# The first product of a channel MLP by one level of Strassen's algorithm, on chunks of 768 tokens

## The chip, the cores and the metric

The kernel runs on one core of a Trainium2 chip. A core has a matrix engine (TensorE, PE in the profile, with its weight loads as PEld), a vector engine (VectorE, DVE), a scalar engine (ScalarE, ACT), GpSimd (POOL) and a queue that issues transfers (SyncE, SP). Matmuls write to PSUM, which has eight banks of 512 floats per partition; everything else works in SBUF; DMA moves data between SBUF and HBM. The metric is the time of one execution on the device in microseconds (us), the median of several.

## The reference

The kernel computes attention, a gated mixer and a channel MLP for 4 batches of 576 tokens with 512 channels. The change concerns the MLP, which comes last (x is the output of the mixer):

```
mu = np.mean(x, axis=-1, keepdims=True)
var = np.mean((x - mu) ** 2, axis=-1, keepdims=True)
xn = (x - mu) / np.sqrt(var + 1e-06) * g_ln
ch = np.maximum(xn @ w_ch1, 0.0) @ w_ch2
return (x + ch).astype(np.float32)
```

w_ch1 is 512 x 2048 and w_ch2 2048 x 512. The weights arrive as 64-bit floats.

## The kernel before

Batches go through four segments each: "v" (5 steps), "u", "g" and "y" (8 steps each), in the order of `order` (L833). In g the gating product ps_g is multiplied with u (L569) and split (L570, L571); in y the output product ps_y gets its residual (L588) and goes to `y_scratch` in HBM (L590). A table of hooks places other work in front of a step: `hook(b, seg, i, fn)`. In the last batch these are weight pieces for the MLP (WA_AT, WC_AT) and the statistics of its first chunk (NORM0_AT). A hook gives a place in the written order, not a time: the framework's scheduler follows that order as a priority and may put a ready instruction of a later step before one that waits. On the chip each engine then keeps the order that it was given.

Every large product is made from float32r parts. `split` (L175) writes a high part on ACT and the rest on DVE, and `mm3` (L202) issues three matmuls for each 128 x 128 weight block: low by high, high by low, high by high. A weight load belongs to each matmul.

Weights are converted from 64 bits by `from_f64` (L184): ACT takes the scaled absolute value of the high word, DVE shifts it, puts the sign in (L194) and ORs the low word's bits (L196). Nine of the 32 pieces (PRE) are converted in an earlier batch and kept in `w_scratch`; `load_w` (L624) fetches or converts a piece and splits it into w1 or w2 tiles, which stay in SBUF for all chunks. g_ln is multiplied into w1 there.

The MLP has its tokens in five chunks (CUTS): two of 384, three of 512. `norm` (L658) has four steps for a chunk: load and sum over channels (step 0), subtract the mean and split into xn (1), the variance (2) and its inverse root, which is kept in rb (2 or 3). `ch1` (L736) makes one block of 128 features (4 blocks of channels by 3 matmuls, then Relu on ACT, L748, and the rest on DVE, L749), `ch2_mm` (L752) adds it to four accumulators, and `ch2_out` (L760) multiplies by rb, adds the residual and stores. The second product runs two blocks behind the first (LAG). For the first two chunks the features go in two halves, so that the later weights can be prepared meanwhile:

```
    todo = [(c, f, r, r + hh - 1) for r in (0, hh) for c in (0, 1) for f in range(r, r + hh)]
    todo += [(c, f, 0, NF - 1) for c in range(2, NCHUNK) for f in range(NF)]
```

PSUM: two banks hold ps_h, two the statistics, four the accumulators.

Of the kernel before, what the change touches and what calls it, by code (L numbers as in the profile page):

```python
# [24 lines left out]
P = 128  # L25
# [15 lines left out]
CUTS = (0, 384, 768, 1280, 1792, 2304)  # L41
CM = 512
NT = B * S
WP = 512
# [3 lines left out]
LAG = 2  # L48
# [10 lines left out]
WA_AT = (("u", 2), ("u", 2), ("u", 6), ("g", 2), ("g", 4), ("g", 5))  # L59
NORM0_AT = (("g", 0), ("g", 5), ("y", 5), ("y", 7))  # L60
WC_AT = (2, 5, 6, 6)
NORM1_AT = (1, 2, 6, 7)
NORM2_AT = (10, 11, 14, 15)
NORMC_AT = (5, 6, 9, 11)
# [3 lines left out]
PRE = (7, 8, 18, 21, 22, 24, 25, 28, 30)  # L68
# [12 lines left out]
NCHUNK = len(CUTS) - 1  # L81
TPC = CUTS[1] // P
# [65 lines left out]
def mixer_kernel(ctx: ExitStack, tc: tile.TileContext, io, out):  # L148
    nc = tc.nc
    y_d = nc.dram_tensor("y_scratch", (KD, P, NT), F32, kind="Internal").ap()  # L150
    w_d = nc.dram_tensor("w_scratch", (len(PRE), P, WP), F32, kind="Internal").ap()
    pools = {}
# [31 lines left out]
    def from_f64(raw, w, src, k, queue=nc.sync, after=None):  # L184
# [409 lines left out]
    wstage = []  # L594
# [25 lines left out]
    def from_pre(w, n):  # L620
        nc.sync.dma_start(out=w.bitcast(F32), in_=w_d[n])
        return w.bitcast(F32)

    def load_w(pl, i, j):  # L624
        k = wseq.index((i, j))
        w = wstage[0].tile([P, WP], U32, tag="w", name="w")
        if k in PRE:
            f = from_pre(w, PRE.index(k))
        else:
            raw = wstage[0].tile([P, 2 * WP], U32, tag="raw", name="raw")  # L630
            f = from_f64(raw, w, w_src(i, j), 2).rearrange("p k f -> p (k f)")
        if j < 2:
            if j == 0:
                w1[i] = pl.tile([P, 2, KD, 256], F32R, name=f"w1_{i}")
            kk = 2 * j
            f = f.rearrange("p (k f) -> p k f", k=2)
            for n in range(2):
                split(w1[i][:, 0, kk + n, :], w1[i][:, 1, kk + n, :], f[:, n, :],
                      scale=g_2[:, kk + n:kk + n + 1])
        else:  # L640
            if j == 2:
                w2[i] = pl.tile([P, 2, 2, DM], F32R, name=f"w2_{i}")
            j -= 2
            split(w2[i][:, 0, j, :], w2[i][:, 1, j, :], f)

    ys, xns, rbs, hs, accs = {}, {}, {}, {}, {}

    nst = {}

# [238 lines left out]
```

## Time and profile before

| | |
|---|---|
| median of 3 runs | 703.49 us (702.27 to 705.4) |
| the profiled execution, first to last instruction | 706.4 us |
| PE busy in it | 686.8 us, 97% |
| DVE, ACT busy | 59%, 40% |
| bytes moved by DMA | 61.25 MB |
| first matmul of the MLP | 300.66 us |

The profile is of one execution, which lies 0.4% above the median of the runs shown. Times in its rows count from the first instruction. Matmuls overlap: the distance between their starts tells what one costs, their listed duration includes the time that results take to come out. PE at 97% says that PE hardly waits, not that its matmuls could not be fewer.

### The profile page before, as it was taken

Reading aid. Unit: us, or ns where it says so; the run is one execution under the profiler, and the core shown is the slowest. Engines: PE = TensorE matmul, PEld = TensorE weight load, DVE = VectorE, ACT = ScalarE, POOL = GpSimd, SP = SyncE. Lnnn points to the kernel's source line nnn. Section 1 sums busy time; section 2 is a strip of 40 time slices with the busy share of each in tenths; the row PEclk is TensorE's granted clock in tenths of the full one; section 3 lists DMA queues with packets and bytes.
Section 4 is the critical chain, followed back from the end, with each engine's and each line's share of the span. In section 5 each row is a group of like instructions: output and inputs, shape, how many; then the busy total and the mean of one; then the engine's idle time right before and its main releaser. Section 6 shows DMA issues by size and latency. Waiting matters only on the chain.

```text
span 706.4 us, 11932 instructions
## 1 busy us (share of the span) xinstructions
PE 686.8 (97%) x4818; PEld 613.9 (87%) x4818; DVE 414.9 (59%) x866; ACT 280.9 (40%) x723; POOL 25.5 (4%) x26
## 2 busy tenths in 40 slices
PE   5999999999999999999999999999999999999997
PEld 4779979989998999999999999888888888888885
DVE  4889797696877894898963145656115461141113
ACT  3878966392578453465531114132111321111110
POOL 0012011000200020000000000000000000000000
PEclk9999999999999999999999999999999999999999
DMA  8764233457343524154420030300003000010001
GB/s 266 246 191 143 82 94 112 154 159 226 112 131 105 146 82 156 59 154 153 150 90 1 0 105 1 104 1 1 0 1 119 1 1 0 1 61 0 1 0 60
DMA packets 29240, 61.25 MB, mean 87 GB/s; under 512 B 3009, under 2 KB 10177, under 8 KB 29185
## 3 DMA queue, kind: packets, MB, share of 16 engines
q1 hardware_dynamic: 29184, 60.49, 27.2%
q8 instruction: 38, 0.62, 0.4%
q14 instruction: 18, 0.14, 0.1%
HBM read 48.68 MB, written 11.80 MB: 86 GB/s over the span
## 4 chain that ended last, share of the span: by engine, by line
PE 72%; DVE 10%; ACT 8%; DMA 6%; issue 1%; POOL 1%; SPq 1%; ACTq 0%; POOLq 0%; DVEq 0%
PE ps_h L205 9%; PE ps_h L203 9%; PE ps_h L204 9%; PE ps_o L203 8%; PE ps_o L204 8%; PE ps_o L205 8%; DMA w_scratch<-w_p 3%; ACT pt L400 2%; PE ps_y L203 2%; DMA yT<-y_scratch 2%; PE ps_y L204 2%; PE ps_y L205 2%; PE ps_t L439 1%; PE ps_v L203 1%; PE ps_pv L458 1%
## 5 line engine op out<-in xcount | busy, mean ns | idle before, releaser
L749 DVE SCALAR_TENSOR_TENSOR h<-ps_h,h 128x512 fp32r<-128x512 f32 (+1 forms) x80 | 50.6, 632 | 181.3 <-ACT h L748 181.2
L748 ACT ACTIVATE h<-ps_h 128x512 fp32r<-128x512 f32 (+1 forms) x80 | 44.3, 553 | 235.4 <-PE ps_h L205 230.0
L203 PE MATMUL ps_o<-h,w 128*128 128x512 f32 (+1 forms) x320 | 117.5, 368 | 0.3 <-DVE o L763 0.3
L203 PE MATMUL ps_h<-xn,w 128*128 128x512 f32 (+1 forms) x320 | 117.6, 367 | 0.0
L204 PE MATMUL ps_h<-xn,w 128*128 128x512 f32 (+1 forms) x320 | 117.5, 367 | 0.0
L205 PE MATMUL ps_h<-xn,w 128*128 128x512 f32 (+1 forms) x320 | 117.5, 367 | 0.0
L205 PE MATMUL ps_o<-h,w 128*128 128x512 f32 (+1 forms) x320 | 117.5, 367 | 0.0
L204 PE MATMUL ps_o<-h,w 128*128 128x512 f32 (+1 forms) x320 | 117.5, 367 | 0.0
L203 PEld LDWEIGHTS ps_o<-h,w 128*128 128x128 f32 x320 | 60.1, 188 | 8.6 <-DVE o L763 1.0
L204 PEld LDWEIGHTS ps_o<-h,w 128*128 128x128 f32 x320 | 60.0, 188 | 7.6
L205 PEld LDWEIGHTS ps_h<-xn,w 128*128 128x128 f32 x320 | 60.1, 188 | 7.5
L205 PEld LDWEIGHTS ps_o<-h,w 128*128 128x128 f32 x320 | 60.1, 188 | 7.5
L204 PEld LDWEIGHTS ps_h<-xn,w 128*128 128x128 f32 x320 | 60.1, 188 | 7.4
L203 PEld LDWEIGHTS ps_h<-xn,w 128*128 128x128 f32 x320 | 60.1, 188 | 7.4
L203 PE MATMUL ps_g<-wsg,vn 128*128 128x288 f32 x128 | 39.2, 307 | 0.3 <-ACT wsg L177 0.3
L203 PE MATMUL ps_y<-gt,wout 128*128 128x288 f32 x128 | 38.0, 298 | 1.1 <-ACT gt L570 1.1
L205 PE MATMUL ps_g<-wsg,vn 128*128 128x288 f32 x128 | 38.3, 300 | 0.0
L203 PE MATMUL ps_u<-xhl,winl 128*128 128x288 f32 x128 | 38.1, 297 | 0.0
L204 PE MATMUL ps_g<-wsg,vn 128*128 128x288 f32 x128 | 37.8, 296 | 0.0
L204 PE MATMUL ps_y<-gt,wout 128*128 128x288 f32 x128 | 37.7, 295 | 0.0
L205 PE MATMUL ps_u<-xhl,winh 128*128 128x288 f32 x128 | 37.7, 295 | 0.0
L205 PE MATMUL ps_y<-gt,wout 128*128 128x288 f32 x128 | 37.7, 295 | 0.0
(171 smaller groups left out, 1277.2 us busy)
## 6 DMA issues: line engine op xcount, KB each, us to landing
raw<-in_w_ch SPq DMA_DIRECT2D x23, 512.0 KB, 3.9
qk<-in_qk_s SPq DMA_DIRECT2D x8, 601.0 KB, 4.8
raw_p<-in_w_ch SPq DMA_DIRECT2D x18, 256.0 KB, 3.1
y_scratch<-y SPq DMA_DIRECT2D x16, 288.0 KB, 3.4
qk<-in_qk_l SPq DMA_DIRECT2D x7, 592.0 KB, 4.9
st<-in_w_in SPq DMA_DIRECT2D x8, 512.0 KB, 6.0
vt<-in_v_l SPq DMA_DIRECT2D x8, 432.0 KB, 5.4
vt<-in_v_s SPq DMA_DIRECT2D x8, 384.0 KB, 3.2
```

The lines of the kernel that those rows point to most:

```text
L203: nc.tensor.matmul(ps, lhsT=ll, rhs=rh, start=first, stop=False)
L204: nc.tensor.matmul(ps, lhsT=lh, rhs=rl, start=False, stop=False)
L205: last_mm[0] = nc.tensor.matmul(ps, lhsT=lh, rhs=rh, start=False, stop=last)
L400: exps.append(nc.scalar.activation(p3[:, i, :], src, AF.Exp, scale=SCALE, bias=mx[:, i:i + 1], accum_out=sm[:, i:i + 1]))
L439: nc.tensor.transpose(ps[:rows, (t - t0) * c:(t - t0 + 1) * c], src, ident)
L458: nc.tensor.matmul(ps[64 * h:64 * h + 64, (i - b0) * QB:(i - b0 + 1) * QB], lhsT=vt[:LW, (i * 2 + h) * D:(i * 2 + h + 1) * D], rhs=pT[:LW, ...
L748: nc.scalar.activation(h[:, 0, :], o, AF.Relu)
L749: nc.vector.scalar_tensor_tensor(out=h[:, 1, :], in0=o, scalar=0.0, in1=h[:, 0, :], op0=ALU.max, op1=ALU.subtract)
```

## The change

The tokens come in three chunks of 768 (TC), each in two halves of 384 (TH); a pair of feature blocks (256 columns of w_ch1) is the unit of the first product. The 512 channels are two halves as well, so that one pair is a 2 x 2 by 2 x 2 block product, and Strassen's algorithm (in Winograd's form) makes it from seven products of half the contraction instead of eight. WX names which of seven weight operands and which of seven token operands each product takes. `combine` makes the weight operands of a pair with four additions and three splits, `expand` the token operands with four subtractions and seven splits. `pair` issues the products in the order 1, 6, 2, 7, 4, 5, 3, adds them up on DVE, and gives the two blocks of the first half at once (h1, h2) and the two of the second half as sums kept in SBUF (`late`), whose Relu and second product come in a loop after the eight pairs. The second product of the first half stands between the products of the next pair.

w1 operands are 3.5 blocks of 512 columns in two parts, 1792 KB a pair, and only two pairs fit: each pair is written to `w1_scratch` once (`keep`) and read again for the second and third chunk (`fetch`). g_ln is now multiplied into the tokens (norm step 5). The inverse root is worked out with one reciprocal and a Newton step (`rsqrt`). The sign of the 64-bit weights comes from Prelu's slope, which saves one DVE operation in every conversion. Other pieces are converted early (PRE), and the hooks of the last batch change (PREP_AT, NORM0_AT). Banks: the pairs' products use one set of four banks, the accumulators of the first half the other, and the sets change places from chunk to chunk (role).

```diff
-CUTS = (0, 384, 768, 1280, 1792, 2304)
-CM = 512
+TC, TH = 768, 384
...
+WX = {1: (0, 0), 2: (1, 1), 7: (2, 5), 4: (3, 2), 5: (4, 3), 6: (5, 4), 3: (6, 6)}
...
-WA_AT = (("u", 2), ("u", 2), ("u", 6), ("g", 2), ("g", 4), ("g", 5))
-NORM0_AT = (("g", 0), ("g", 5), ("y", 5), ("y", 7))
...
+PREP_AT = (("u", 2, 2), ("u", 6, 1), ("g", 2, 2), ("g", 4, 1), ("g", 5, 2), ("y", 2, 1), ("y", 4, 2), ("y", 6, 1))
+NORM0_AT = (("g", 0, "n", 0), ("g", 3, "n", 1), ("g", 4, "n", 2), ("g", 6, "n", 3), ("g", 7, "n", 4), ("y", 1, "n", 5),
+            ("y", 2, "e", 0), ("y", 2, "e", 1), ("y", 3, "e", 2), ("y", 4, "e", 3), ("y", 5, "e", 4), ("y", 6, "e", 5),
+            ("y", 7, "e", 6))
+NORM_AT = ({6: (0, 1), 7: (2, 3, 4, 5)}, {2: (0,), 3: (1,), 4: (2,), 5: (3,), 6: (4,), 7: (5,)})
+EXPAND_AT = (0, 1, 3, 5, 6, 8, 10)
...
-PRE = (7, 8, 18, 21, 22, 24, 25, 28, 30)
+PRE = (8, 9, 12, 13, 16, 17, 20, 21, 24)
...
+    w1_d = nc.dram_tensor("w1_scratch", (NW, P, 14 * 2 * P), F32, kind="Internal").ap()
...
-        first = nc.scalar.activation(wf, high.bitcast(F32), AF.Abs, scale=F64_SCALE)
+        first = nc.scalar.activation(wf, high.bitcast(F32), AF.Prelu, scale=F64_SCALE, alpha=F64_SIGN)
...
         nc.vector.tensor_scalar(out=w, in0=w, scalar1=3, scalar2=None, op0=ALU.logical_shift_left)
-        nc.vector.scalar_tensor_tensor(out=w, in0=high, scalar=0x80000000, in1=w,
-                                       op0=ALU.bitwise_and, op1=ALU.bitwise_or)
         nc.vector.scalar_tensor_tensor(out=w, in0=low, scalar=29, in1=w,
                                        op0=ALU.logical_shift_right, op1=ALU.bitwise_or)
...
+    def piece(i, j):
...
         if k in PRE:
-            f = from_pre(w, PRE.index(k))
+            nc.sync.dma_start(out=w.bitcast(F32), in_=w_d[PRE.index(k)])
...
+            r0 = 1024 * (piece_turn[0] % 2)
+            piece_turn[0] += 1
+            from_f64(stg[:, r0:r0 + 1024], w, w_src(i, j), 2)
...
+    def combine(i):
...
+        tt(out=s[:, 0], in0=a21, in1=a22, op=ALU.add)
+        tt(out=s[:, 1], in0=s[:, 0], in1=a11, op=ALU.subtract)
+        tt(out=a21, in0=a11, in1=a21, op=ALU.subtract)
+        tt(out=s[:, 2], in0=a12, in1=s[:, 1], op=ALU.subtract)
+        w = w1[i] = big["w1", i % 2].tile([P, 2, 7, 2, P], F32R, tag="w1", name=f"w1_{i % 2}")
+        for src, j, m in ((wf[:, :, 0:P], 0, 2), (wf[:, :, P:2 * P], 2, 2), (s.rearrange("p s k f -> p (s k) f"), 4, 3)):
+            split(w[:, 0, j:j + m].rearrange("p s k f -> p (s k) f"), w[:, 1, j:j + m].rearrange("p s k f -> p (s k) f"),
+                  src)
...
+    def keep(i):
+        nc.sync.dma_start(out=w1_d[i], in_=w1[i].rearrange("p a s k f -> p (a s k f)").bitcast(F32))
+    def fetch(i):
+        w = w1[i] = big["w1", i % 2].tile([P, 2, 7, 2, P], F32R, tag="w1", name=f"w1_{i % 2}")
+        nc.sync.dma_start(out=w.rearrange("p a s k f -> p (a s k f)").bitcast(F32), in_=w1_d[i])
...
+    def second(i):
...
+        w = w2[i] = big["w2", i].tile([P, 2, 2, DM], F32R, name=f"w2_{i}")
+        split(w[:, 0].rearrange("p k f -> p (k f)"), w[:, 1].rearrange("p k f -> p (k f)"), f)
...
+    units = [(fn, a) for i in range(NW) for fn, a in (
+        (piece, (i, 0)), (piece, (i, 1)), (combine, (i,)), (piece, (i, 2)), (piece, (i, 3)), (second, (i,)))]
+    done = [0]
+    def prepare(n):
+        for fn, a in units[done[0]:done[0] + n]:
+            fn(*a)
+        done[0] += n
...
+    def bank(role, name):
+        if role:
+            return ps_d.tile([P, 512], F32, tag="d", name=name)
+        turns[0] += 1
+        if turns[0] % 2:
+            return ps_s.tile([P, 512], F32, tag="s", name=name)
+        return ps_a.tile([P, 512], F32, tag="a", name=name)
...
+    def norm(sc, step, role):
...
+            n = big["norm", 0] if sc == 0 else big["yc"].tile([P, KD * TC], F32, tag="yc", name="yc")
+            yc = ys[sc] = n[:, :KD * TC].rearrange("p (k t) -> p k t", k=KD)
+            nc.sync.dma_start(out=yc, in_=y_d[:, :, sc * TC:(sc + 1) * TC].rearrange("k p t -> p k t"))
...
+        if step in (1, 2):
+            half = step - 1
...
+            sr = col_sum(sc, half, False)
+            mean = bank(role, "ps_m")[:, :TH]
...
+                out=yc[:, :, cs], in0=mean.unsqueeze(1).to_broadcast([P, KD, TH]), scalar=-1.0 / DM,
+                in1=yc[:, :, cs], op0=ALU.mult, op1=ALU.add)
+        elif step in (3, 4):
+            half = step - 3
+            sr = col_sum(sc, half, True)
+            o = bank(role, "ps_v2")[:, :TH]
...
+            nc.scalar.activation(rbs[sc][:, half, :], o, AF.Identity, scale=1.0 / DM, bias=eps)
...
+            for k in range(KD):
+                nc.scalar.activation(yc[:, k, :], yc[:, k, :], AF.Copy, scale=g_2[:, k:k + 1])
...
+    def rsqrt(sc, half):
...
+        nc.scalar.activation(t, ve, AF.Sqrt)
+        nc.vector.reciprocal(r, t)
+        nc.scalar.activation(t, r, AF.Square)
+        nc.vector.tensor_tensor(out=t, in0=t, in1=ve, op=ALU.mult)
+        nc.vector.tensor_scalar(out=t, in0=t, scalar1=-0.5, scalar2=1.5, op0=ALU.mult, op1=ALU.add)
+        nc.vector.tensor_tensor(out=ve, in0=r, in1=t, op=ALU.mult)
...
+    def expand(sc, step):
+        yc = ys[sc]
+        b11, b12, b21, b22 = yc[:, 0:2, :TH], yc[:, 0:2, TH:], yc[:, 2:4, :TH], yc[:, 2:4, TH:]
...
+        def put(j, src):
+            x = xns[sc, j] = big["x"].tile([P, 2, 2, TH], F32R, tag=f"x{j}", name=f"x{j}")
+            split(x[:, 0], x[:, 1], src)
+        if step == 0:
+            put(0, b11)
+            tt(out=b11, in0=b12, in1=b11, op=ALU.subtract)
+        elif step == 1:
+            put(6, b22)
+            tt(out=b12, in0=b22, in1=b12, op=ALU.subtract)
         elif step == 2:
...
+            tt(out=b22, in0=b22, in1=b11, op=ALU.subtract)
+            put(4, b22)
+        elif step == 3:
+            put(1, b21)
+            tt(out=b21, in0=b22, in1=b21, op=ALU.subtract)
+        elif step == 4:
+            put(5, b12)
+        elif step == 5:
+            put(2, b21)
+        else:
+            put(3, b11)
+    def product(sc, i, o, m, first):
+        wj, xj = WX[m]
+        w, x = w1[i], xns[sc, xj]
+        for k in range(2):
+            for n, (a, c) in enumerate(((1, 0), (0, 1), (0, 0))):
+                nc.tensor.matmul(o, lhsT=w[:, a, wj, k, :], rhs=x[:, c, k, :], start=first and k == 0 and n == 0,
+                                 stop=k == 1 and n == 2, skip_group_check=True)
...
+    def to_h(src):
...
+    def ch2(sc, half, f, role, f0=0, f1=NF - 1, ds=range(KD)):
...
+    def leave(sc, half, d):
...
+        r = big["tmp"].tile([P, TH], F32, tag="o", name="o", bufs=2)
+        nc.vector.tensor_tensor(out=r, in0=accs[half, d][:, :TH], in1=rbs[sc][:, half, :], op=ALU.mult)
+        y = ys.pop((sc, half, d))
         nc.vector.tensor_tensor(out=y, in0=r, in1=y, op=ALU.add)
...
+        nc.sync.dma_start(out=out[d, :, cs], in_=y)
...
+    def pair(sc, i, role):
+        tt = nc.vector.tensor_tensor
+        f1, f2 = 2 * i, 2 * i + 1
+        a = bank(role, "ps_p1")[:, :TH]
+        product(sc, i, a, 1, True)
+        s1 = tmp("s1")
+        nc.scalar.activation(s1, a, AF.Copy)
+        b = bank(role, "ps_p6")[:, :TH]
+        product(sc, i, b, 6, True)
+        u2 = tmp("u2")
+        tt(out=u2, in0=b, in1=s1, op=ALU.add)
+        product(sc, i, a, 2, False)
+        h1 = to_h(a)
+        d = bank(role, "ps_p7")[:, :TH]
+        product(sc, i, d, 7, True)
+        u3 = tmp("u3")
+        tt(out=u3, in0=d, in1=u2, op=ALU.add)
+        if i:
+            ch2(sc, 0, f1 - 2, 1 - role)
+        e = bank(role, "ps_p4")[:, :TH]
+        product(sc, i, e, 4, True)
+        c21 = tmp("c21")
+        tt(out=c21, in0=u3, in1=e, op=ALU.subtract)
+        h2 = to_h(c21)
+        c = bank(role, "ps_p5")[:, :TH]
+        product(sc, i, c, 5, True)
+        tt(out=late(f2), in0=c, in1=u3, op=ALU.add)
+        if i:
+            ch2(sc, 0, f2 - 2, 1 - role)
+        product(sc, i, c, 3, False)
+        tt(out=late(f1), in0=c, in1=u2, op=ALU.add)
+        hs[f1], hs[f2] = h1, h2
+    def last_stage():
+        for sc in range(NSC):
+            role = sc % 2
+            for i in range(NW):
+                pair(sc, i, role)
+                if sc == 0:
+                    if i + 2 < NW:
+                        prepare(len(units[done[0]:]) if i + 3 == NW else 6)
+                        if i < NW - 2:
+                            keep(i + 2)
+                elif i + 2 < NW:
+                    fetch(i + 2)
+                if sc + 1 < NSC:
+                    for step in NORM_AT[sc > 0].get(i, ()):
+                        norm(sc + 1, step, role)
+                if i == NW - 3:
+                    residual(sc, 0)
+                if i >= NW - 2:
+                    rsqrt(sc, i + 2 - NW)
+            for f in (NF - 2, NF - 1):
+                ch2(sc, 0, f, 1 - role)
+            for d in range(KD):
+                leave(sc, 0, d)
+            if sc + 1 < NSC:
+                fetch(0)
+                fetch(1)
+            for f in range(NF):
+                hs[f] = to_h(late(f))
+                if sc + 1 < NSC and f in EXPAND_AT:
+                    expand(sc + 1, EXPAND_AT.index(f))
+                if f == 4:
+                    residual(sc, 1)
+                if f < NF - 2 or sc + 1 < NSC:
+                    ch2(sc, 1, f, role)
+            for d in range(KD):
+                if sc + 1 == NSC:
+                    for f in (NF - 2, NF - 1):
+                        ch2(sc, 1, f, role, ds=(d,))
+                leave(sc, 1, d)
...
     def open_c():
         close("mid")
...
+        right("x")
...
+    for seg, i, n in PREP_AT:
+        hook(last, seg, i, prepare, n)
+    for seg, i, what, step in NORM0_AT:
+        if what == "n":
+            hook(last, seg, i, norm, 0, step, 0)
+        else:
+            hook(last, seg, i, expand, 0, step)
+    hook(last, "y", 7, keep, 0)
...
+    open_d()
+    prepare(max(0, 12 - done[0]))
+    keep(1)
+    last_stage()
...
```

## Rows read from the trace of the kernel before

**Rows 1.** The page: the head and part 1, busy us, share and instructions.

```profile
span 706.4 us, 11932 instructions
PE 686.8 (97%) x4818; PEld 613.9 (87%) x4818; DVE 414.9 (59%) x866; ACT 280.9 (40%) x723; POOL 25.5 (4%) x26
```

**Rows 2.** Busy time by stretch: PE, PEld, DVE, ACT, POOL, PE clock, DMA share, GB/s.

```profile
269.00:278.00 9.00, 9.00 (x71) 9.00 (x70) 3.05 (x7) 1.30 (x3) 0.00 (x0) 1.00 0.61 206
...
285.50:300.66 15.16, 14.09 (x106) 13.85 (x105) 13.88 (x34) 7.27 (x13) 1.05 (x1) 1.00 0.23 79
300.66:360.00 59.34, 59.00 (x342) 58.36 (x341) 54.83 (x108) 33.29 (x62) 1.29 (x1) 1.00 0.49 156
360.00:700.00 340.00, 338.94 (x1597) 293.12 (x1597) 121.02 (x159) 61.38 (x92) 0.00 (x0) 1.00 0.06 22
```

**Rows 3.** Timeline of PE, first and last of three runs: start, duration, instruction.

```profile
292.07 0.29 PE L203 MATMUL ps_y<-gt,wout 128*128 128x288 f32 x1
...
294.05 0.30 PE L203 MATMUL ps_y<-gt,wout 128*128 128x288 f32 x1
...
307.28 0.33 PE L203 MATMUL ps_o<-h,w 128*128 128x384 f32 x1
...
311.44 0.33 PE L203 MATMUL ps_o<-h,w 128*128 128x384 f32 x1
...
690.10 0.39 PE L203 MATMUL ps_o<-h,w 128*128 128x512 f32 x1
...
695.54 0.39 PE L203 MATMUL ps_o<-h,w 128*128 128x512 f32 x1
```

**Rows 4.** Groups by line and shape, weight loads: count, busy us, mean ns, idle.

```profile
L203 PEld LDWEIGHTS ps_h<-xn,w 128*128 128x128 f32 x320 | 60.1, 188 | 7.4
```

**Rows 5.** Waits of PE: us in total, times, longest.

```profile
PE ps_m L673 <- DVE sr L178: 2.0, 2, 1.1
...
PE ps_y L203 <- ACT gt L570: 1.1, 1, 1.1
```

**Rows 6.** Timeline of DVE as the first chunk's tokens arrive.

```profile
276.33 0.56 DVE L653 TENSOR_TENSOR s<-yT 128x384 f32<-128x384 f32 x1 [2.84 <-DMA yT<-y_scratch]
276.80 0.55 DVE L654 TENSOR_TENSOR s<-yT 128x384 f32<-128x384 f32 x1
277.27 0.45 DVE L571 TENSOR_TENSOR gt<-z,gt 128x288 fp32r<-128x288 f32 x1
277.64 0.55 DVE L655 TENSOR_TENSOR s<-s,s 128x384 f32<-128x384 f32 x1
...
281.33 1.75 DVE L676 SCALAR_TENSOR_TENSOR xc<-ps_m,yT 128x1536 f32<-128x1536 f32 x1
283.00 0.45 DVE L571 TENSOR_TENSOR gt<-z,gt 128x288 fp32r<-128x288 f32 x1
```

**Rows 7.** Groups by line and shape: sign operation, reciprocal, table loads.

```profile
L194 DVE SCALAR_TENSOR_TENSOR w<-raw,w 128x512 uint32<-128x512 uint32 x23 | 15.8, 686 | 0.2
...
L699 DVE RECIPROCAL rb<-sd 128x512 f32<-128x512 f32 x3 | 10.1, 3353 | 10.0 <-ACT sd L696 10.0
...
L288 ACT ACT_TABLE_LOAD x5 | 6.4, 1283 | 0.1
```

**Rows 8.** Timeline: last matmul of a block, its Relu, its rest.

```profile
404.71 0.33 PE L205 MATMUL ps_h<-xn,w 128*128 128x384 f32 x1
...
405.08 0.49 ACT L748 ACTIVATE h<-ps_h 128x384 fp32r<-128x384 f32 x1 [3.67 <-PE ps_h L205]
...
405.60 0.56 DVE L749 SCALAR_TENSOR_TENSOR h<-ps_h,h 128x384 fp32r<-128x384 f32 x1 [3.60 <-ACT h L748]
```

**Rows 9.** DMA issues: count, KB each, median us from issue to landing.

```profile
yT<-y_scratch SPq DMA_DIRECT2D x3, 1024.0 KB, 5.0
...
yT<-y_scratch SPq DMA_DIRECT2D x2, 768.0 KB, 8.1
```

**Rows 10.** Timeline of SP, issues of the first two token loads.

```profile
269.05 0.93 SPq L664 DMA_DIRECT2D yT<-y_scratch  x2
```

More of the change, by code (lines that the diff above doesn't have):

```diff
@@ new lines, in acc_bank, with scratch, col_sum @@
+    def acc_bank(role, d):
+        if role:
+            return ps_d.tile([P, 512], F32, tag="d", name="ps_o")
+        if d < 2:
+            return ps_s.tile([P, 512], F32, tag="s", name="ps_o")
+        return ps_a.tile([P, 512], F32, tag="a", name="ps_o")
+    def scratch(sc, n):
+        if sc:
+            return big["tmp"].tile([P, TH], F32, tag="o", name="o", bufs=2)
+        return big["norm", 0][:, KD * TC + n * TH:KD * TC + (n + 1) * TH]
+    def col_sum(sc, half, square):
+        yc = ys[sc]
+        s, t = scratch(sc, 0), scratch(sc, 1)
+        cs = slice(half * TH, (half + 1) * TH)
+        tt = nc.vector.tensor_tensor
+        if square:
+            nc.scalar.activation(s, yc[:, 0, cs], AF.Square)
+            for k in range(1, KD):
+                nc.scalar.activation(t, yc[:, k, cs], AF.Square)
+                tt(out=s, in0=s, in1=t, op=ALU.add)
+        else:
+            tt(out=s, in0=yc[:, 0, cs], in1=yc[:, 1, cs], op=ALU.add)
+            tt(out=t, in0=yc[:, 2, cs], in1=yc[:, 3, cs], op=ALU.add)
+            tt(out=s, in0=s, in1=t, op=ALU.add)
+        sr = big["sr"].tile([P, 2, TH], F32R, tag="sr", name="sr")
+        split(sr[:, 0, :], sr[:, 1, :], s)
+        return sr
@@ new lines, in product @@
+    def product(sc, i, o, m, first):
[6 more added lines that the diff above has]
+    def to_h(src):
+        h = big["h"].tile([P, 2, TH], F32R, tag="h", name="h")
+        nc.scalar.activation(h[:, 0, :], src, AF.Relu)
+        nc.vector.scalar_tensor_tensor(out=h[:, 1, :], in0=src, scalar=0.0, in1=h[:, 0, :],
+                                       op0=ALU.max, op1=ALU.subtract)
+        return h
@@ L810, in open_c, with open_d @@
-        wc.append(pool("wc", side="right", reuse_waits="tile"))
+        right("x")
+        right(("w2", 2))
+    def open_d():
+        close("dn", "dw", "cw")
+        for i in range(3, NW):
+            right(("w2", i))
+        right("h", 3)
+        right("tmp")
+        right("ev")
+        right("lt")
+        right("yc")
+        big["late", 0] = big["nm"].tile([P, NLATE, TH], F32, tag="n0", name="late")
+        big["late", 1] = big["lt"].tile([P, NF - NLATE, TH], F32, name="late2")
     last = B - 1
@@ L813, in mixer_kernel @@
     hook(last, "v", 0, open_a)
-    for k, (seg, i) in enumerate(WA_AT):
-        hook(last, seg, i, lambda k=k: load_w(wa[0], *wseq[k]))
     hook(last, "g", 0, open_b)
-    for step, (seg, i) in enumerate(NORM0_AT):
-        hook(last, seg, i, lambda step=step: norm(0, step, nm[0], xa[0]))
     hook(last, "y", 0, open_c)
-    for k in range(6, 10):
-        hook(last, "y", WC_AT[k - 6], lambda k=k: load_w(wc[0], *wseq[k]))
+    for seg, i, n in PREP_AT:
+        hook(last, seg, i, prepare, n)
```

245 lines of the change are left out of this document (70 added, 175 removed).

## The prediction

> **What bounds the kernel now.** I read the head of the page first, then busy time by stretch, then the waits of TensorE, and only then single instructions. TensorE (PE) is busy for 97% of 706.4 us; VectorE (DVE) for 59%, ScalarE (ACT) for 40% [rows 1]. The stretches show the kernel's two lives: the channel MLP, from 300.66 us to the end, keeps PE busy for 59.00 of 59.34 us and then 338.94 of 340.00, at a granted clock of 1.00, the 2.4 GHz level, in every row [rows 2]. No other engine holds the end there; late in the MLP, DVE is idle for two thirds of the time. But where the MLP begins DVE is nearly full: 13.88 of 15.16 us before it, 54.83 of 59.34 after [rows 2]. So the MLP is priced by PE's instructions, and the risk sits around 270 to 360 us, on DVE.
>
> The price of a matmul is the distance between starts, not its duration (they overlap). From 307.28 to 311.44 us stand 24 matmuls of 384 columns: 0.1733 us each. From 690.10 to 695.54 stand 24 of 512: 0.2267 us [rows 3]. The difference gives 0.416 ns per column and 13.4 ns per matmul.
>
> **What goes: columns.** Before, the first product costs 2304 tokens x 16 feature blocks x 4 x 3 = 442,368 columns, in 960 matmuls; the second as many. Of these 1920, 768 are 384 wide (133.1 us) and 1152 are 512 wide (261.1 us): 394.2 us. After, a pair of feature blocks takes 7 products x 2 x 3 = 42 matmuls, so 3 chunks x 8 pairs x 42 = 1008, beside 1152 of the second product, all 384 wide: 2160 x 0.1733 = 374.4 us. **Net -19.8 us**: 55,296 columns are worth 23.0, and 240 more instructions give 3.2 back. The statistics' matmuls inside the MLP go from 4 of 384 and 12 of 512 (3.4 us; the six tiny ones beside them left out) to 16 of 384 (2.8): -0.6.
>
> Weight loads speak against this. One lasts 188 ns [rows 4], longer than 173 ns, and their number rises to 2160. "Perfetto Trace Analysis" of the Trainium skill, section "Identifying the Most-Contended Engine", would judge TensorE by the LDWEIGHTS busy share rather than by matmul time. By that rule weight loads would bound the MLP at 2160 x 0.188 = 406 us, and nothing would be won. The trace disagrees: 15 matmuls of 288 columns with their loads start within 1.98 us, 132 ns each [rows 3], so loads of 188 ns overlap too.
>
> **What comes, 1: the first chunk's inputs.** The first chunk grows from 384 to 768 tokens and is normalised and split into seven operands before the MLP starts. DVE takes one result per 1.04 ns plus 0.07 us: 384 elements per 0.47 us, 1536 per 1.67 [rows 6]; so 0.34 for 256, 0.60 for 512, 0.87 for 768. Before, two token loads of 768 KB were issued together at 269.05 us [rows 10], median 8.1 us to landing [rows 9]; the new one of 1536 KB is the same bytes, so all is there near 278. From then DVE owes: two halves of sums, splits, mean and squares (8 x 0.47 + 1.67 each: 10.8 us), 4 subtractions and 7 splits of 768 (11 x 0.87 = 9.6), the gating and output operations still due (16 x 0.37 = 6), and what is left of the weights' preparation, say 4 (DVE has 6 us free from 269 to 278 to do the rest [rows 2]). Sum 30.4: done at 308.4, near 310 with ACT's halves in between. PE wants its first product at 300.7 and its sixth, whose operand comes last, at 305.9. I take **4.5 us**; 0 if the queue order favours the operands, 10 if the output stage is held up too. Nothing else can fill PE there.
>
> **2: preparing weights in the first chunk.** Per pair DVE owes 7 results of 384 (3.3 us), four additions of 256 and three splits for w1 (3.4), a split of 1024 for w2 (1.1) and two conversions (1.9, one operation less than before, which cost 0.68 [rows 7]): 9.7 of the 66 x 0.1733 = 11.44 us that PE takes; 10.6 and 11.6 for the last two sets, which convert three and four pieces, and statistics of the next chunk follow. On the SP queue a write-back of 1792 KB waits for the last split, with the next pieces behind it; per pair 3.4 MB move, 298 GB/s, where 206 GB/s took 0.61 of the DMA engines [rows 2], so 338 in full. DVE was as full before, and PE lost 0.34 us [rows 2]; but then a result had 4 us to arrive. Now the third product waits on a short chain. After the fourth product's last start come 0.37 us to ACT or DVE (404.71 to 405.08) and 0.5 us for each step [rows 8]: subtraction, Relu, rest, addition, together 2.5 us, hidden behind product 5 and 12 matmuls, 3.1 us. 0.6 us of slack is less than one 768-wide operation in the way. I take 0.5 us for each of seven pairs: **3.5**; between 0 and 8.
>
> **3: openings of the chunks.** Pair 0 has no second product to hide behind, so the chain leaves 1.3 us bare; the next pair's first product fits in if the order allows. The framework's order does put ready work of other steps between (a gating operation stands between two additions of one sum [rows 6]). Half of 3 x 1.3, rounded down: **1.5**; 0 to 5. The four exits of a chunk (8 x 0.47 us on DVE) stand ahead of the next pair's results, hidden by its five products (5.2 us) in four free banks; without them the same chain is bare.
>
> **4: at nothing.** Twelve reloads of 1792 KB, each issued when its buffer's last reader is done and needed one pair later, 11.44 us: 1024 KB took 5.0 us [rows 9], so at most 8.8; at the rate of the crowded pair of loads 9.5. Two reciprocals per chunk (3.35 us at 512 [rows 7], so about 2.5 each) stand in the last pairs, needed 4 us after; late, they would hold the exits and so the second half's banks. Fewer DVE operations in the attention stages: no wait of PE there names a conversion, so nothing; at most 1 us. The longest waits after the start, for statistics and gating [rows 5], I leave as they are.
>
> **The sum.** -19.8 - 0.6 + 4.5 + 3.5 + 1.5 = -10.9: the profiled execution would go from 706.4 to 695.5 us. The median of runs is 703.49, 0.9959 of that span (the page gives no other time of its own), so **692.5 us**.
>
> **The rivals.**
> *All new work is hidden* (0.20). The three losses together cost 0 to 4 us: 683 to 687. For it: DVE at 92% cost PE 0.34 us before. Against: the chain's small slack, and inputs due at 300.7.
> *The first chunk goes at the pace of DVE or the queue* (0.14). A start 10 us late and 0.8 to 1.2 us in each pair: losses of 14 to 22, so 697 to 705. For it: 9.7 to 11.6 us of DVE work in 11.44.
> *The chain is bare in every pair* (0.07), in all chunks, and this one is slower. Where PE's order puts the third product before the 12 matmuls, or each step takes longer than 0.5 us, PE stands still 24 times. With the late start, 0.66 us each eats the gain, 0.81 makes it slower than can be mistaken; at 1.3 us it is 31 us: 719. Against: the written order has cover for 3.1 us.
> *Reloads late* (0.05). If 1792 KB take over 11.44 us, each us costs 12: 1 us late gives about 704. Rows of 5.0 and 8.1 us speak against it.
> *Weight loads bound PE* (0.02): 406 us for an MLP of 401, some 708; the 132 ns speak against it. *ACT loads tables for the new Prelu* (0.02): 34 conversions stand among Gelu and Exp, two loads of 1.283 us each [rows 7], 87 us of ACT in stages of 400 us; some 30 us slower. "ScalarE: Activation LUTs" of the Trainium skill, section "Table sets: the hidden batching unit", says that cheap functions are in every set and names relu, copy, identity and abs; no run here shows Prelu.
>
> **How the numbers follow.** The forecast has 0.50 and its own range, losses of 4 to 14 us, is 687 to 698. The range takes in most of the hidden case below and half of the first-chunk case above: **682 to 701**, leaving out the slower cases and the rest, 2 in 10. A difference of 0.5% (3.5 us) is about what can be told from none: below 700.0 lie the forecast, the hidden case, half of the first-chunk case and part of the reloads, 0.80; within, 0.10; above, the bare chain, the tables, part of the others, 0.10.
>
> **What would show it.** PE's starts 0.173 us apart and 2160 matmuls in the MLP (step one); PE waiting for a split of the x tiles at about 300 to 312 us, 3 to 6 us in sum (1); waits for the late tiles or free banks in the first chunk, under 1 us a pair (2), and almost none in the others; no PE wait for reloads (4). The prediction falls if these waits recur in the second and third chunk, if the output stage before 300 us stretches, or if the granted clock leaves 1.00 there: then waiting costs twice.

## The result, and the profile after

The changed kernel takes 698.88 us (median of 4 runs, 698.06 to 700.12), the kernel before beside it 704.44 (702.27 to 706.59): a ratio of 0.9915, interval 0.9885 to 0.9944, faster by 0.85%. The profiled span goes from 706.4 us [rows 1] to 697.5. In every run that has both numbers the time is 1.7 to 1.9 us more than the span (699.26 for 697.5 here); a span of 706.4 would be a time of about 708.2, above all four runs of the kernel before. So its profile lies above its runs, and the 8.9 us between the two profiles are more than the 5.6 us between the medians. The head of its page, part 1 and the clock by slices:

```profile
span 697.5 us, 12744 instructions
PE 672.5 (96%) x5050; PEld 642.9 (92%) x5050; DVE 474.0 (68%) x992; ACT 319.0 (46%) x803; POOL 21.0 (3%) x24
PEclk9899999999999999999999979999999999999999
```

Busy time by stretch, from the first matmul of the first product (298.71 us); columns as in [rows 2]:

```profile
298.71:310.00 11.29, 9.09 (x40) 7.60 (x39) 11.29 (x19) 6.21 (x10) 0.00 (x0) 0.85 0.16 49
310.00:396.00 86.00, 85.65 (x492) 85.00 (x491) 79.55 (x147) 41.75 (x70) 0.00 (x0) 1.00 0.78 274
396.00:420.00 24.00, 17.87 (x74) 16.18 (x74) 19.12 (x30) 15.39 (x26) 0.00 (x0) 0.79 0.26 98
420.00:460.00 40.00, 40.00 (x232) 39.84 (x231) 22.25 (x42) 8.52 (x16) 0.00 (x0) 1.00 0.42 145
...
620.00:660.00 40.00, 40.00 (x233) 40.00 (x232) 13.59 (x26) 5.58 (x11) 0.00 (x0) 1.00 0.26 93
```

From 420 us on PE is full, at 0.172 to 0.173 us a matmul: the price per matmul was right, and the second and third chunk lose nothing. What is lost is a stretch less its matmuls at 0.1733 us: 4.4 us up to 310 (40 matmuls in 11.29), 0.7 in the pairs of the first chunk (492 in 86.00), **11.2 in the seam of the first chunk** (74 in 24.00), the stretch between its pairs and those of the second. From the first product to the last matmul (693.10) 394.4 us pass; 2176 matmuls are 377.1; so 17.3 are lost. The three places give 16.3; the rest is counting, since a matmul that crosses an edge is in both rows.

The start, in PE's timeline (a row with x23 is a run of 23):

```profile
298.71 1.21 PE L783 MATMUL ps_p<-x,w 128*128 128x384 f32 x6
300.42 0.45 PE L783 MATMUL ps_p<-x,w 128*128 128x384 f32 x1 [0.51 <-ACT x L179]
302.02 5.94 PE L783 MATMUL ps_p<-x,w 128*128 128x384 f32 x23 [1.16 <-ACT x L179]
...
308.50 6.64 PE L783 MATMUL ps_p<-x,w 128*128 128x384 f32 x36 [0.54 <-DVE u L839]
```

Three waits, 2.2 us, two of them for splits of x, and a run at 0.258 us a matmul, part of it at the lower clock. The seam, in the same view:

```profile
397.61 0.45 PE L732 MATMUL ps_v<-sr,one 128*128 128x384 f32 x1 [0.74 <-DVE sr L180]
...
403.21 0.44 PE L732 MATMUL ps_v<-sr,one 128*128 128x384 f32 x1 [1.75 <-DVE sr L180]
...
407.03 0.52 PE L204 MATMUL ps_o<-h,w 128*128 128x384 f32 x1
407.35 0.52 PE L205 MATMUL ps_o<-h,w 128*128 128x384 f32 x1
...
412.34 2.29 PE L783 MATMUL ps_p<-x,w 128*128 128x384 f32 x6 [3.06 <-DVE o L821]
415.21 0.69 PE L783 MATMUL ps_p<-x,w 128*128 128x384 f32 x1 [0.58 <-ACT s L835]
...
416.01 0.52 PE L205 MATMUL ps_o<-h,w 128*128 128x384 f32 x1
416.33 0.52 PE L204 MATMUL ps_o<-h,w 128*128 128x384 f32 x1
```

PE first waits twice for the column sums of squares of the second chunk; then the second chunk's first product waits 3.06 us for a bank that an exit (`leave`, L821) has to empty. After that matmuls start 0.32 us apart (416.01, 416.33): the granted clock is at its lower level, 1.2 GHz, until 418.25; it is 0.79 in the stretch's mean. It had been there once before, from 404.79 to 407.99 (407.03, 407.35). The four waits are 6.1 of the 11.2 us; the 25 or so matmuls at 0.32 instead of 0.173 us make up, by count, another 3.7. Why the exits are late stands in DVE's timeline:

```profile
402.60 0.56 DVE L180 TENSOR_TENSOR sr<-o,sr 128x384 fp32r<-128x384 f32 x1 [0.68 <-ACT sr L179]
403.83 2.55 DVE L745 RECIPROCAL o<-o 128x384 f32<-128x384 f32 x1 [0.68 <-ACT o L744]
...
407.91 0.56 DVE L747 TENSOR_TENSOR o<-o,rb 128x384 f32<-128x384 f32 x1 [0.71 <-ACT o L746]
...
410.39 0.56 DVE L749 TENSOR_TENSOR rb<-o 128x384 f32<-128x384 f32 x1
...
411.73 1.02 DVE L821 TENSOR_TENSOR o<-ps_o,rb 128x384 f32<-128x384 f32 x2
```

Between the sums and the first exit stands the whole inverse root of the *second* half (403.83 to 410.39, with input work of the next chunk between its links), which nothing needs before that half leaves. DVE isn't full there (19.12 of 24 us): it waits for ACT between links, and what stands behind waits too.

The reloads are hidden, as DMA issues after 300 us (count, KB each, median us to landing) and PE's waits show, none of which names a DMA:

```profile
w<-w_scratch SPq DMA_DIRECT2D x16, 1792.0 KB, 7.4
```

### The profile page after: what moved, and what is told of

Same layout as the page of the kernel before. It is cut to its first block, busy times and chain, and to the rows that moved or that the text cites. A ratio compares the mean times of both kernels' runs of the same rounds, so it can differ in the third digit from the quotient of the medians.

```text
span 697.5 us, 12744 instructions
## 1 busy us (share of the span) xinstructions
PE 672.5 (96%) x5050; PEld 642.9 (92%) x5050; DVE 474.0 (68%) x992; ACT 319.0 (46%) x803; POOL 21.0 (3%) x24
## 4 chain that ended last, share of the span: by engine, by line
PE 75%; DVE 10%; ACT 8%; DMA 5%; issue 1%; SPq 1%; ACTq 0%; DVEq 0%
PE ps_p L783 21%; PE ps_o L205 9%; PE ps_o L204 8%; PE ps_o L203 8%; PE ps_u L203 2%; PE ps_u L205 2%; PE ps_u L204 2%; PE ps_v L203 2%; PE ps_v L204 2%; PE ps_v L205 2%; PE ps_y L203 2%; PE ps_y L205 2%; PE ps_y L204 2%; ACT pt L400 2%; PE ps_t L439 1%
## 5 line engine op out<-in xcount | busy, mean ns | idle before, releaser
L783 PE MATMUL ps_p<-x,w 128*128 128x384 f32 x1008 | 188.2, 339 | 6.2 <-DVE o L821 3.1
L783 PEld LDWEIGHTS ps_p<-x,w 128*128 128x128 f32 x1008 | 177.3, 190 | 9.4 <-DVE o L821 3.4
L204 PE MATMUL ps_o<-h,w 128*128 128x384 f32 x384 | 129.7, 338 | 0.0
L205 PE MATMUL ps_o<-h,w 128*128 128x384 f32 x384 | 129.4, 338 | 0.0
L203 PE MATMUL ps_o<-h,w 128*128 128x384 f32 x384 | 128.6, 336 | 0.0
L205 PEld LDWEIGHTS ps_o<-h,w 128*128 128x128 f32 x384 | 73.3, 191 | 0.0
L204 PEld LDWEIGHTS ps_o<-h,w 128*128 128x128 f32 x384 | 73.1, 190 | 0.1
L203 PEld LDWEIGHTS ps_o<-h,w 128*128 128x128 f32 x384 | 72.6, 189 | 0.2
L789 DVE SCALAR_TENSOR_TENSOR h<-late,h 128x384 fp32r<-128x384 f32 x48 | 26.5, 558 | 47.4 <-ACT h L788 47.4
L788 ACT ACTIVATE h<-late 128x384 fp32r<-128x384 f32 x48 | 25.2, 525 | 68.0 <-PE ps_o L205 68.0
L204 PE MATMUL ps_u<-xhl,winh 128*128 128x288 f32 x128 | 37.8, 295 | 0.0
L205 PE MATMUL ps_u<-xhl,winh 128*128 128x288 f32 x128 | 37.7, 295 | 0.0
L788 ACT ACTIVATE h<-c 128x384 fp32r<-128x384 f32 x24 | 12.6, 523 | 51.4 <-DVE c L851 51.3
L835 ACT ACTIVATE s<-ps_p 128x384 f32<-128x384 f32 x24 | 11.7, 489 | 49.7 <-PE ps_p L783 49.6
L203 PE MATMUL ps_v<-winh,xhl 128*128 128x512 f32 x80 | 32.2, 403 | 0.2 <-DVE xhl L495 0.2
```

The lines of the kernel that those rows point to most:

```text
L203: nc.tensor.matmul(ps, lhsT=ll, rhs=rh, start=first, stop=False)
L204: nc.tensor.matmul(ps, lhsT=lh, rhs=rl, start=False, stop=False)
L205: last_mm[0] = nc.tensor.matmul(ps, lhsT=lh, rhs=rh, start=False, stop=last)
L783: nc.tensor.matmul(o, lhsT=w[:, a, wj, k, :], rhs=x[:, c, k, :], start=first and k == 0 and n == 0, stop=k == 1 and n == 2, skip_group_che ...
L788: nc.scalar.activation(h[:, 0, :], src, AF.Relu)
L789: nc.vector.scalar_tensor_tensor(out=h[:, 1, :], in0=src, scalar=0.0, in1=h[:, 0, :], op0=ALU.max, op1=ALU.subtract)
```

## The experiments

Each ratio is to the kernel before, run on the same chip. The first matmul of the first product starts anywhere between 296.4 us (experiment 8) and 300.66 (the kernel before) in these profiles, not by the edits alone: the first 40 us differ from one execution to the next. So "MLP" below is the span less that start: 405.7 us before (706.4 less 300.66), 398.8 after. Each MLP is from one profile. In 11 and 12 the clock fell in the seam (0.93 over 24 us) where in 1, with the same code there, it stayed at 1.00, which was worth some 1.4 us; so differences of up to 2 us are not read as effects.

| experiment | ratio, interval | span | MLP |
|---|---|---|---|
| changed kernel | 0.9915, 0.9885 to 0.9944 | 697.5 | 398.8 |
| 1 late inverse root | 0.9797, 0.9782 to 0.9812 | 689.5 | 392.6 |
| 2 exits without scratch | 0.9832, 0.9814 to 0.985 | 693.7 | 396.3 |
| 3 both roots in the last pair | 0.9935, 0.992 to 0.995 | 698.5 | 401.4 |
| 4 sums from pair 4 | 0.9831, 0.9811 to 0.9852 | 691.5 | 394.5 |
| 5 sums from pair 5 | 0.9836, 0.9802 to 0.9871 | 689.2 | 392.1 |
| 6 an eighth product | 1.0248, 1.0221 to 1.0275 | 721.0 | 422.7 |
| 7 old conversion | 0.9891, 0.9868 to 0.9913 | 695.4 | 397.5 |
| 8 Prelu alone in the kernel before | 1.0044, 1.0025 to 1.0062 | 706.7 | 410.3 |
| 9 split of w2 later | 0.9836, 0.9804 to 0.9869 | 690.8 | 393.4 |
| 10 first chunk normalised earlier | 0.9836, 0.9822 to 0.9851 | 690.9 | 394.0 |
| 11 start filled with matmuls | 0.9819, 0.979 to 0.9848 | 694.0 | 394.6 |
| 12 reloads twice | 0.9987, 0.9959 to 1.0015 | 701.9 | 403.4 |

4, 5, 7 and 9 to 12 are built on 1 and stand against its 0.9797.

**1. The inverse root moved out of the seam.**

```diff
-                if i >= NW - 2:
-                    rsqrt(sc, i + 2 - NW)
+                if i == NW - 2:
+                    rsqrt(sc, 0)
...
+                if f == 10:
+                    rsqrt(sc, 1)
```

> The second half's inverse square root of a chunk is moved from its last pair into the loop of the second half (behind fragment 10); nothing else is changed. Theory A (the exits of the first half wait for the two shared scratch tiles, which this inverse root passes through behind the next chunk's statistics): the wait of the next chunk's first product for a bank (3.06 us, released by the exits) goes, and with it part of the clock loss at the seam of the first chunk; the span falls from 697.5 to about 691 to 694 us, some 0.986 of the time of the kernel before. The waits of 0.74 and 1.75 us for the statistics stay. Theory B (VectorE simply has more work between the pairs and the second half of the first chunk than that stretch has time): the work is only put later, about the same total waits and the same span of 696 to 699 us, ratio 0.991.

DVE's timeline, the first exit and the moved reciprocal, and the seam's 24 us by stretch:

```profile
400.84 0.56 DVE L821 TENSOR_TENSOR o<-ps_o,rb 128x384 f32<-128x384 f32 x1
...
418.11 2.55 DVE L745 RECIPROCAL o<-o 128x384 f32<-128x384 f32 x1
```

```profile
394.20:418.20 24.00, 20.50 (x114) 19.27 (x114) 21.05 (x35) 17.55 (x31) 0.00 (x0) 1.00 0.40 137
```

The exit comes 10.9 us sooner (9.1 counted from the first product, which starts at 296.89), the wait of 3.06 us is gone, the clock stays at 1.00 and 114 matmuls start where 74 did: 6.9 us by count. The MLP is 6.2 us shorter, and only the root was moved: theory A. Its span of 691 to 694 us was undercut by the earlier start. The waits left in the seam are 0.74, 2.17 and 0.58 us, 2.6 less than before; the other 3.6 us of the gain came with the clock.

**2. Exits in place in their bank**, so that they need no scratch tile:

```diff
-        r = big["tmp"].tile([P, TH], F32, tag="o", name="o", bufs=2)
+        r = accs[half, d][:, :TH]
```

> The exits multiply by the inverse root in place in their PSUM bank and need no scratch tile any more; the order of the instructions on VectorE is the scheduler's own and may stay. Theory A in its narrow form (the scratch tiles alone hold the exits back): the first exit comes before the inverse root of the second half, about 5 us sooner, the wait of 3.06 us goes; span 691 to 694 us. If instead the order in which VectorE is given its work holds them back: exits at the same place behind the inverse root, wait stays near 3 us, span 696 to 699 us. Theory B: the same, 696 to 699 us.

The first exit is at 395.77, the wait for it gone; but the exits now stand in front of the column sums, whose two waits grow from 2.5 to 4.6 us. PE's waits (us in total, times, longest):

```profile
PE ps_v L732 <- DVE sr L180: 4.6, 2, 3.2
```

The MLP gains 2.5 us, no more. So the scratch tiles are what tied the exits to the root, but early exits alone are not the cure: with the root's own 4.0 us of DVE still in the seam 2.5 us are won, with the root out of it (1) 6.2. Both edits together were not tried.

**3. The opposite**: in the changed kernel both inverse roots are given out in the last pair (`if i == NW - 1: rsqrt(sc, 0); rsqrt(sc, 1)`).

> From the changed kernel itself, the opposite of the late inverse root: the first half's inverse root of a chunk is given out in the last pair too, right in front of the second half's. Theory A (the exits are held by what stands between them and the end of the pairs in VectorE's order): the first exit, which needs the first half's root, comes about 4 us later, the next chunk's first product waits 6 to 8 us instead of 3.06 us, and more of the seam is at the lower clock: span 701 to 706 us. Theory B (only the sum of VectorE's work in the seam counts): a root taken out of a pair and put in the seam adds its own 4.4 us of work there at most, but the pairs gain the same: 697 to 700 us.

The first exit comes at 416.14, 4.4 us later (6.1 counted from the first product, at 297.05), and PE stands for 6.8 us, if on another instruction than I named:

```profile
412.41 0.69 PE L204 MATMUL ps_o<-h,w 128*128 128x384 f32 x1 [6.76 <-DVE h L789]
```

The order of events is A's: what stands in front in DVE's queue holds up what PE needs. The time does not decide: the MLP grows by 2.6 us, where I expected 4 to 9, the span of 698.5 us lies in B's 697 to 700, and the ratio's interval overlaps that of the changed kernel. B's other half is not there, though: the pairs gain nothing, PE's waits in them are 0.8 us against 0.4.

**4 and 5. The statistics spread over more pairs** (first entry of NORM_AT `{4: (0,), 5: (1,), 6: (2, 3), 7: (4, 5)}`, then `{5: (0,), 6: (1, 2), 7: (3, 4, 5)}`, in place of `{6: (0, 1), 7: (2, 3, 4, 5)}`).

> On top of the late inverse root: in the first chunk the steps of the second chunk's statistics are given out from pair 4 (load), 5, 6 and 7 instead of 6 and 7. Theory A (the two waits of TensorE at the column sums of squares, 0.74 and 2.17 us with the late inverse root, come from ScalarE's and VectorE's work being given out late): they fall below 1 us in all, span 686.5 to 688.5 us. Theory B (VectorE has too much work in that stretch, 19 to 22 of 24 us): the waits only go elsewhere, into the pairs that still prepare weights, span 689 to 691 us.

> On top of the late inverse root: a milder form of the earlier statistics, steps 0 in pair 5, 1 and 2 in pair 6, 3 to 5 in pair 7 of the first chunk. If only the number of steps crowded into pair 7 makes the waits at the column sums (2.9 us), they fall by some 1 to 2 us without new waits in pairs 5 and 6: span 687.5 to 689 us. If VectorE's and ScalarE's work in the stretch sets the sum of the waits, it stays: 689 to 691 us.

In 4 the waits for sums fall to 1.4 us, and a wait of 2.3 us for a split of h takes their place; in 5 they stay at 2.9. No gain either time, as theory B has it: as far as two orders show, with the root gone what is left of the seam is the work of DVE and ACT, not its place.

**6. An eighth product**: product 4 is issued twice in every pair and only the second counts, no other engine having more to do.

> One of the seven products of every pair is issued twice into the same bank (six matmuls of 384 columns more in each of the 24 pairs, 144 in all), with no additions of any other engine; this is the number of products that the form without Strassen has. The product counted is then the same one twice over, overwritten, so only the time is changed. If TensorE bounds every pair, it costs 144 x 0.1733 = 25.0 us: span 722 us, ratio 1.027. If the pairs were bound by VectorE or by the chain of additions, part of it would be hidden: under 20 us, ratio below 1.02.

The MLP grows by 23.9 us, 0.96 of 25.0. So a saved product is worth its TensorE time, and the pairs are not bound by DVE. Against the kernel before, with as many columns to multiply, all else that the change brings costs 2.5%.

**7 and 8. The sign by Prelu, undone in the new kernel and alone in the old one.**

```diff
-        first = nc.scalar.activation(wf, high.bitcast(F32), AF.Prelu, scale=F64_SCALE, alpha=F64_SIGN)
+        first = nc.scalar.activation(wf, high.bitcast(F32), AF.Abs, scale=F64_SCALE)
...
+        nc.vector.scalar_tensor_tensor(out=w, in0=high, scalar=0x80000000, in1=w,
+                                       op0=ALU.bitwise_and, op1=ALU.bitwise_or)
```

> On top of the late inverse root: the conversion of the weights is put back to its old form (Abs, and one VectorE instruction more, about 0.68 us by its sister in the same conversion). Some 14 conversions fall into the pairs of the first chunk, where VectorE is busy 78 of 86 us: 9.5 us more work. If VectorE sets the pace of the first chunk once it is full (the rival on the first chunk): waits of TensorE in those pairs of 2 to 6 us, span 692 to 697 us. If there is room (my forecast priced these pairs at 0.5 us each and the trace showed 0.4 us in all): below 1 us, span 689 to 691 us.

> The kernel before with only the new conversion of the weights (Prelu with a power of two as its negative slope carries the sign; one VectorE instruction less in each). If Prelu lies in the function table that stands anyway, and VectorE has the slack that the rows show: no difference, ratio 0.997 to 1.003. If Prelu asked for a table of its own, each of the conversions between GELUs would load tables twice: many rows of table loads and several us to some tens of us slower. If VectorE bounds the stretches with the conversions: some us faster.

In the new kernel the old form costs 4.9 us of MLP. The stretch and PE's waits there:

```profile
340.00:396.00 56.00, 53.77 (x297) 52.02 (x295) 54.45 (x100) 26.35 (x45) 0.00 (x0) 0.97 0.69 256
```

```profile
PE ps_p L785 <- DVE w L180: 2.0, 1, 2.0
...
PE ps_o L205 <- DVE w L180: 1.5, 1, 1.5
PE ps_p L785 <- DVE late L857: 1.2, 1, 1.2
```

DVE is busy for 54.45 of 56 us and PE waits for weights: the cause that the rival on the first chunk names appears one DVE operation away, though as three waits from 387 to 400 us and not as 0.8 to 1.2 us in each pair. In the kernel before Prelu takes 25 us off DVE (414.9 to 389.7) and wins nothing, slightly loses (0.4%; the MLP is 4.6 us longer); PE's waits for rests of h (2.3 us) and an exit (1.6) appear where the MLP begins. Why that order got worse I did not follow. Eleven table loads in both, at 1283 ns each [rows 7]: no extra table for Prelu.

**9 and 10. The start.** The split of the second piece of w2 is taken away from in front of the inputs (`("y", 6, 1)` out of PREP_AT); and the first chunk's normalisation and inputs are given out one to two groups earlier (NORM0_AT).

> On top of the late inverse root: the split of the second piece of w_ch2 (1.22 us of VectorE, which stands between the splits that make the first chunk's inputs) is taken out of the preparation before the first chunk and put into its first pair. Theory A (the start waits for VectorE's queue of splits and additions, what stands among them is paid for): the waits of TensorE in the first 10 us of the first product, 2.1 us with the late inverse root, fall by about 1 us, and the granted clock of 0.83 there may rise; span 687 to 689 us against 689.5. Theory B (the start is a chain that goes through ScalarE and VectorE in turn, with room between its links): no difference, 689 to 690 us, or the work is missed later in the pairs.

> On top of the late inverse root: the steps that normalise the first chunk and make its seven inputs are given out one to two groups earlier in the last matmul groups of the token mixing; no instruction is added or removed. Theory A (the start of the first product waits because the chain of input splits is begun late): its three waits, 2.1 us in all, fall below 1 us and the granted clock of 0.83 in the first 10 us rises; span 685.5 to 688.5 us. Theory B (VectorE is at work without a gap from 269 to 309 us, so the chain ends when its work ends, whatever the order): no gain, span 689 to 691 us, or waits in the token mixing instead.

Neither helps: waits of 2.2 and 3.6 us against 2.1, and the first matmul of the second product, with 66 before it, comes 17.3 and 18.2 us after the first product's first (297.37, 296.94), against 16.3 in 1 (296.89). It is this row in 1, 9 and 10:

```profile
313.18 0.33 PE L203 MATMUL ps_o<-h,w 128*128 128x384 f32 x1
...
314.66 0.33 PE L203 MATMUL ps_o<-h,w 128*128 128x384 f32 x1
...
315.11 0.33 PE L203 MATMUL ps_o<-h,w 128*128 128x384 f32 x1
```

In 10 the stretch ahead of the start shows why:

```profile
290.00:300.00 10.00, 8.59 (x59) 7.80 (x57) 9.72 (x15) 9.97 (x16) 0.00 (x0) 1.00 0.52 176
```

ACT is busy for 9.97 of 10 us, DVE for 9.72. The inputs' work can't be had before the tokens come, and then both engines are full: its sum sets when the inputs are there, as in B. The last split of x ends 8.2 us after the first product's first matmul, as in 1. Experiment 9 is another case. There DVE has less to do and the last split of x ends sooner, 7.1 us after; but only DVE's part of the moved split went behind the inputs, ACT's part (298.01, 1.05 us) still stands between two of them, and the second input comes later. Then the clock, in 1 and in 9:

```profile
300.00:310.00 10.00, 9.37 (x41) 8.33 (x42) 10.00 (x20) 4.15 (x8) 0.00 (x0) 0.83 0.32 96
...
300.00:310.00 10.00, 9.03 (x34) 8.38 (x35) 8.10 (x13) 3.60 (x6) 0.00 (x0) 0.66 0.39 117
```

From 301.93 on PE waits for no input in 9, yet the row has 34 matmuls against 41, at a mean clock of 0.66 instead of 0.83, and DVE, full in 1, is busy for 8.10 of 10 us. What came sooner was lost at the lower clock.

**11. The waits of the start filled**: the very first product is issued three times, so that PE has useless work instead of waits.

```diff
-        product(sc, i, a, 1, True)
+        for _ in range(3 if (sc, i) == (0, 0) else 1):
+            product(sc, i, a, 1, True)
```

> On top of the late inverse root: the very first product of the first chunk is issued three times over into the same bank (twelve matmuls more, 2.08 us of TensorE's time, overwritten and without effect on the result), where TensorE otherwise waits 0.54, 1.15 and 0.40 us for the splits of its next operands. Theory A (the waits cost twice, since the clock falls to its lower level after them): the waits are filled, the granted clock in the first 10 us stays at 1.00 instead of 0.83, and some 1.5 to 2 us that the half clock took are won: span 687.5 to 688.5 us against 689.5, although TensorE has more to do. Theory B (the fall of the clock has another cause, or costs nothing since the operands come late anyway): no gain, or up to 2 us lost: span 689.5 to 691.5 us.

```profile
300.00:310.00 10.00, 8.36 (x44) 7.08 (x42) 10.00 (x17) 5.64 (x9) 0.00 (x0) 1.00 0.12 36
```

The clock stays at 1.00, and nothing is won. PE merely waits later (0.42, 0.68, 0.54 us), and the first matmul of the second product comes 16.3 us after the first product's first (299.42), as in 1, with 78 matmuls before it instead of 66:

```profile
315.68 0.34 PE L203 MATMUL ps_o<-h,w 128*128 128x384 f32 x1
...
396.70:420.70 24.00, 20.51 (x106) 19.43 (x105) 19.91 (x33) 17.12 (x30) 0.00 (x0) 0.93 0.40 136
```

So 12 useless matmuls fit into the waits and into what the lower clock had taken. Theory B, with its second reason: here the lower clock costs nothing of its own, since the operands come no sooner (the last split of x ends 8.3 us after the start). The MLP is 2.0 us longer all the same, but not there: the seam (second row) has 106 matmuls at a clock of 0.93, where 1 has 114 at 1.00, and a wait of 0.72 us at 446.77 has no counterpart in 1. Nothing in the edit touches these places.

**12. Every reload fetched twice** into its tile.

> On top of the late inverse root: each of the 16 reloads of combined weights (1792 KB) is fetched twice over, 28.7 MB more. If the reloads are hidden (each takes 7.4 us to landing and a pair lasts some 16 us): no difference, span 689 to 691 us. If they were on the edge: TensorE waits for the DMA at the pairs of the second and third chunk, up to 7 us in each of the 14 that are prepared two pairs ahead.

My 16 us were wrong: a pair lasts 11.44, as the prediction has it, so two reloads of 7.4 us don't fit.

```profile
PE ps_p L784 <- DMA w<-w_scratch: 5.2, 7, 1.1
```

Seven waits on the reload, 5.2 us, where the single one has none; the MLP is 10.8 us longer. Some 1.4 of the rest is the seam, where the clock fell as in 11; the other 4 are not settled. So the reload was hidden with room of some 4 us, less than its own length.

## Why the prediction was right, and where it was off

The forecast was 692.5 us in 682 to 701, the time 698.88: inside the range and on the right side, but 0.9 us outside the likeliest case's own range and, as a number, inside that of the rival on the first chunk (697 to 705), whose mechanism the rows don't show. Between the medians the gain is 5.6 us, half of the 11 forecast. In the span the miss is only 2.0 us (-10.9 forecast, -8.9 measured), and that is luck: 1.95 us of the 8.9 are the earlier start, which differs as much between profiles of the same code. The MLP, which the sum is about, went by -7.0. The rest is the step from span to median. The factor 0.9959 came from one execution's span and other executions' times; within one execution the time is 1.7 to 1.9 us above the span, and the profile of the kernel before lies above its runs.

- **What goes** (-19.8 and -0.6): right. 0.173 us a matmul for two chunks on end; experiment 6 prices the saved product at 0.96 of its matmuls. Weight loads don't bound: PEld is busy for 40.00 of 40.00 us and matmuls of 384 columns still start 0.172 us apart.
- **What comes, 1** (+4.5): right in size, 4.4. The cause is the one named, DVE's and ACT's work after the tokens arrive; experiment 10 moved its order without gain. But PE's waits for x were to be 3 to 6 us in sum and are 1.7, with 0.5 for u; the rest is matmuls at the lower clock, which the sum did not have.
- **2** (+3.5): too much, 0.7. The chain fits into its 3.1 us of cover. But DVE has under 7 us left in 86, and the removed sign operation has its part in that: counted in the 9.7 us a pair, it is worth 4.9 us of MLP (7).
- **3** (+1.5, where half of 3 x 1.3 is 1.95): the step that failed, 11.2 in the first chunk alone. The bare chains themselves are small, waits of 0.54 and 0.58 us in the first and second opening and none in the third. "The four exits of a chunk (8 x 0.47 us on DVE) stand ahead of the next pair's results, hidden by its five products (5.2 us) in four free banks": the next chunk's products take the exits' own banks (role changes), so these are not free. And step 4's "Two reciprocals per chunk", of which it says "late, they would hold the exits", named the mechanism and priced it at nothing, because they are "needed 4 us after". The second one was given out behind the next chunk's statistics, in the exits' scratch tiles, and went first. Moving it gave 6.2 us back (1); adding the other root to it took 2.6 (3), which by itself is not clear of noise. I looked at pairs and openings, and never added up the seam: the last block's results, statistics, a root and the exits in one DVE queue. In the second chunk, where the statistics are spread from pair 2 to 7 and no weights are prepared, the same order costs nothing: the second root's reciprocal starts at 515.66, 18 us before the first exit (533.88), and from 420 us PE does not stand.
- **4**: reloads (16 in all; the 12 counted leave out those in the seams) and tables at nothing, right; the margin of the reloads is some 4 us.
- Left out: losses of 3.2 us inside the MLP of the kernel before (400.8 us from the first matmul to the last, less 397.6), which I carried over by not naming them, and the start, which came 1.95 us earlier (298.71 against 300.66), by chance as far as these profiles tell. The sum by measured terms: matmuls -20.5, losses 17.3 for 3.2, start -1.95, the end after the last matmul -0.6 (4.4 for 5.0): -8.9.
- "If the granted clock leaves 1.00 there: then waiting costs twice": it left 1.00 at the start and in the seam, and only in the seam is it so. At the start experiment 11 held it at 1.00 and won nothing. In the seam the matmuls after 412.34 ran at the lower clock with only one wait, of 0.58 us, behind them; by count the clock cost 3.7 us there beside 6.1 of waits, and with experiment 1 some 3.6 of the 6.2 us came back with it. Holding the clock alone was not tried there.

The first experiment's version beats both kernels: 692.43 us (691.32 to 692.53), 0.9797 of the kernel before.

## What to carry to other kernels

Price the seams between stages as stages of their own: list everything that falls due on each vector engine between the last product of one and the first of the next, in the order in which it was given out, and ask what that product's bank waits for. Work that nothing needs soon (here an inverse root) is moved behind the seam, not merely off the critical path; making a blocked step early without removing the blocker moves the wait. And an edit that only frees an engine with room (one operation less in a conversion) wins nothing alone and is worth 4.9 us once another edit has filled that engine.

## What the hardware showed that I had not expected

After waits of 1 to 3 us the granted clock fell, but not every time: its mean in the first 10 us after 300 was 0.83 in the changed kernel and with the late root, 0.66 in experiments 9 and 10, and 1.00 in experiment 6, with waits of 2.1 to 3.6 us in each. Whether the lower clock costs anything depends on what follows. Where the operands come no sooner, it cost nothing: experiment 11 put 12 matmuls in its place and came out even. Where no wait follows, it did: in the seam of the changed kernel some 3.7 us by count, and in experiment 9 it took what inputs that were ready 1.1 us sooner would have given.
